# Attention and spectral mix on Trainium2: two batches of a head pair as one double unit

## The chip, the core and the metric

The kernel runs on one core of one Trainium2 chip. Its engines work side by side: PE (TensorE) multiplies and transposes, ACT (ScalarE) computes exponentials and copies out of PSUM, DVE (VectorE) multiplies and adds, POOL (GpSimd) casts, and SP (SyncE) issues the DMA transfers. The metric is the device time of one execution in microseconds (us). The median of the runs counts.

## What is computed

Windowed attention with a distance bias, then a mix in the frequency domain, then a residual with a matrix product. Eight batches, eight heads, 576 positions, head size 64, so the model width is 512.

```python
scores = scale * np.matmul(q, k.transpose(0, 1, 3, 2))
mask = (rel >= 0) & (rel < window)            # window = 128
scores = np.where(mask, scores + bias[None], -1000000000.0)
...
attn = attn / (np.sum(attn, axis=-1, keepdims=True) + 1e-09)
attn_out = np.matmul(attn, v)                 # becomes x: batch, position, 512
X = np.fft.rfft(x, axis=1)                    # the first 64 modes are used
Yr = np.einsum('bmd,mde->bme', Xr, w_r) - np.einsum('bmd,mde->bme', Xi, w_i)
Yi = np.einsum('bmd,mde->bme', Xr, w_i) + np.einsum('bmd,mde->bme', Xi, w_r)
y = np.fft.irfft(Y, n=S, axis=1)
u = x + y
out = u + np.maximum(u @ w_ch, 0.0)
```

Each of the 64 modes has its own 512 by 512 matrices w_r and w_i: 134 MB of weights against 28 MB of q, k and v.

## The kernel before

A **unit** is one pair of heads (index s, 0 to 3) of one batch b; there are 32. They go in two groups (GROUPS, line 19): the eight units of pair 0 first, then the 24 of pairs 1 to 3. The weights are split in the same way, by the rows that belong to a group's heads. Group 0's part (22 **weight tiles** of three modes, 768 KB of wr and as much of wi) is multiplied while the second group's attention is still running. The rest is streamed after the attention (lines 177 to 201), and the finish (`_finish`) transforms back and writes the result.

The order of the work on each engine is written by hand: instructions run on every engine in program order. The attention advances by **slots**, calls of `_slot` (lines 534 to 566), numbered n from 0. Slot n does, in this order: the first half of unit n's scores (`_score`, j = 0), the transposes of q and k of unit n+1 (`_tr`) and their copies out of PSUM on ACT (`_evac`), half of the slot's weight tiles (`_modes`), the transposes of unit n-1's v back to rows (`_vnat`, taken by DVE in `_vtake`), the second half of unit n's scores, the transposes of its v, casts to bf16 on POOL for the units to come (`_cast`, `_cast1`), one spectrum step (`_spectrum1`), the product of the weights of unit n-1 with v (`_av`), and the rest of the weight tiles. One score buffer, `sc`, serves both halves, so the second half waits until ACT has taken the exponential of the first. `_keep` (line 416) is a matmul that only keeps PE at work; it opens each unit's scores.

A transpose of q, k or v works on 64 by 64 blocks, one per head, at two positions of the array that can run side by side:

```python
for r in range(g.R):                          # 9
    for hh in range(2):
        hs = slice(64 * hh, 64 * hh + 64)
        g.nc.tensor.transpose(
            tp[hs, r, :], u.b[w][hs, r], g.ident_b[hs, hs], tile_position=(64 * hh, 64 * hh))
```

So a unit has 54 of them, and ten more in `_vnat`. The scores too run in two row halves of the array, one per head (lines 433 to 441).

All loads are issued by SP, in program order; an issue whose buffer is still in use holds up those behind it. q and k have QK = 9 buffers each, v has VB = 6, the weights a ring of RING = 3 tiles. 16 units are asked for ahead of slot 0 (n0, line 113), with the first three weight tiles between them. From slot 8 on, each slot asks for one unit more, then for one weight tile for each that it will use, three ahead (lines 154 to 163). Lines 144 to 153 spread the weight tiles of group 0 over slots 10 to 35: SHARE (4) is a slot's weight up to slot 23, SHARE_END (7) after it. w_ch comes in two loads of 0.5 MB into a buffer of its own (`wcp`, `_load_wch`).

Of the kernel before, what the change touches and what calls it, by code (L numbers as in the profile page):

```python
# [19 lines left out]
LA = 8  # L20
RING = 3
ROWS = 3
VB = 6
VN = 2
QK = 9
# [10 lines left out]
def kernel(  # L36
# [23 lines left out]
    g.units = units = [(j, s, b) for j, grp in enumerate(GROUPS) for b in range(B) for s in grp]  # L60
# [18 lines left out]
    g.W, g.unit, g.acc = {}, {}, {}  # L79
# [11 lines left out]
    with tc.manual_schedule(engines={ET.SP, ET.PE, ET.Activation, ET.DVE, ET.Pool}):  # L91
        with ExitStack() as wctx:
# [4 lines left out]
            with ExitStack() as actx:  # L97
# [4 lines left out]
                g.vns = [cp.tile([P, ST, 2, 72], BF16, name=f"vn{i}") for i in range(VN)]  # L102
                g.qpool = actx.enter_context(tc.tile_pool(name="qk", bufs=QK))
                g.vpool = actx.enter_context(tc.tile_pool(name="v", bufs=VB))
                g.wcp = actx.enter_context(tc.tile_pool(name="wcp", bufs=1))
# [7 lines left out]
                n0 = g.first[1] + LA  # L113
                for n in range(n0):
                    _load_unit(g, n)
                    if n < VB - 1:
                        _load_v(g, n)
                    elif n >= VB + 2:
                        _load_v(g, n - 3)
                    if g.first[1] - 1 <= n < g.first[1] - 1 + RING:  # L120
                        _load_w(g, 0, *todo.pop(0))
                with tc.tile_pool(name="tmpc", bufs=1, side="right") as tp:
                    _consts(g, tp)
                    _cast(g, 0)
                    _cast1(g, 0, 2)
                    _cast(g, 1)
                    for w in range(2):
                        _tr(g, 0, w)
                        _evac(g, 0, w)
                    first = list(dict.fromkeys(u[1] for u in units[:2]))  # L130
                    rest = [s for s in range(NP) if s not in first]
                    for s in first:
                        _mask(g, s)
                    for n in range(3):
                        _slot(g, n, [], [])
                    for s in rest:
                        _mask(g, s)
                zx = ctx.enter_context(tc.tile_pool(name="zx", bufs=1, side="right"))
                g.ZTa = zx.tile([P, 4, 2, NM, 8], FP32)
                loaded = n0  # L140

                line = [(j, *t) for j in range(len(GROUPS)) for t in tiles[j]]
                ahead = RING
                work = {n: [] for n in range(N + 2 + TAIL)}
                for j in range(len(GROUPS) - 1):
                    steps = []
                    for n in range(g.first[j + 1] + 2, g.first[j + 2] + 2):
                        steps += [n] * (SHARE if n < N - LA else SHARE_END)
                    if j + 2 == len(GROUPS):
                        steps += [n for n in range(N + 2, N + 2 + TAIL)] * SHARE_END  # L150
                    steps.sort()
                    for i, t in enumerate(tiles[j]):
                        work[steps[i * len(steps) // len(tiles[j])]].append((j, *t))
                for n in range(3, N + 2 + TAIL):
                    if g.first[1] <= n and loaded < N + 3:
                        if loaded < N:
                            _load_unit(g, loaded)
                        _load_v(g, loaded - 3)
                        loaded += 1
                    w = work[n]  # L160
                    for _ in w:
                        _load_w(g, *line[ahead])
                        ahead += 1
                    h = (len(w) + 1) // 2
                    _slot(g, n, w[:h], w[h:])
                    for i in range(2):
                        if n == g.first[1] + 4 + 8 * i:
                            _load_wch(g, i)
                        if n == g.first[1] + 10 + 8 * i:
                            _cast_wch(g, i)  # L170
# [105 lines left out]
def _mask(g, s):  # L276

    for h in (2 * s, 2 * s + 1):
        g.nc.scalar.activation(g.mask[:, h], g.rel, AF.Exp, scale=-(2.0 ** (-8.0 * (h + 1) / g.H)))
# [47 lines left out]
def _load_unit(g, n):  # L327
    nc = g.nc
    _, s, b = g.units[n]
    u = g.unit.setdefault(n, Ctx())  # L330
    u.q = g.qpool.tile([P, g.R, g.D], FP32, tag="q", name=f"q{n}")
    u.k = g.qpool.tile([P, g.R, g.D], FP32, tag="k", name=f"k{n}")
    for t, src in ((u.q, g.q), (u.k, g.k)):
        nc.sync.dma_start(
            out=t.rearrange("p r d -> p (r d)"),
            in_=src[b, 2 * s : 2 * s + 2].rearrange("h (p r) d -> (h p) (r d)", r=g.R))


def _load_v(g, n):

    _, s, b = g.units[n]
    u = g.unit.setdefault(n, Ctx())
    u.v = g.vpool.tile([P, g.R, g.D], FP32, tag="v", name=f"v{n}")
    g.nc.sync.dma_start(
        out=u.v.rearrange("p r d -> p (r d)"),
        in_=g.v[b, 2 * s : 2 * s + 2].rearrange("h (p r) d -> (h p) (r d)", r=g.R))


def _cast(g, n):
    u = g.unit[n]  # L350
    u.b, u.tp, u.T = [], [], []
    for w in range(2):
        _cast1(g, n, w)


def _cast1(g, n, w):
    u = g.unit[n]
    tb = g.work.tile([P, g.R, g.D], BF16, tag=f"b{w}", name=f"b{w}")
    g.nc.gpsimd.tensor_copy(tb, (u.q, u.k, u.v)[w])  # L359
    u.b.append(tb)  # L360
# [466 lines left out]
```

## Time and profile before

| what | time |
|---|---|
| median of 3 runs | 465.02 us (461.57 to 465.75) |
| the profiled execution | 463.15 us |
| its span, first to last instruction | 461.4 us |
| busy PE / PEld / DVE / ACT / POOL | 344.5 / 232.1 / 223.0 / 201.9 / 104.3 us |
| mean granted clock of PE | 0.748 of full speed |
| read from HBM, written | 163.58 MB, 9.44 MB |

The profile is of one execution. PEld is the loading of a matmul's stationary operand, which overlaps with PE. Busy shares are means over stages with different limits, so the stages have to be read apart. In lists of waits each row is: who waited, for whom, us in total, times, the longest. In the order of time a row is: start, duration, engine, line, operation, result and operands, shape, count, and in brackets how long the engine had been idle and what ended it; "issue" is a wait for nothing that the profile shows. Matmuls overlap one another, so a row of several is shorter than their durations added up.

### The profile page before, as it was taken

The page shows a single profiled execution, that of the slowest core. Times are in us where ns is not written, and L with a number is a line of the kernel's source. Part 1 is how long each engine was busy: PE and PEld are TensorE (multiplying, and loading weights), DVE is VectorE, ACT ScalarE, POOL GpSimd, SP SyncE. Part 2 cuts the span into 40 slices and gives each one's busy share as a digit, 9 for nine tenths or more (in the row PEclk, how much of TensorE's full clock was granted, in tenths as well). Part 3 has the DMA queues.
Part 4 walks back from the last instruction along what each step waited for, and adds up shares of the span by engine and source line. Part 5 has one row for each costly group of instructions (what it writes and reads, how often), then busy time and mean ns, then how long its engine had stood idle before and what let it go on. Part 6 is the DMA issues. An engine that isn't in the chain of part 4 may idle for free.

```text
span 461.4 us, 14063 instructions
## 1 busy us (share of the span) xinstructions
PE 344.5 (75%) x6082; PEld 232.1 (50%) x6110; DVE 223.0 (48%) x444; ACT 201.9 (44%) x316; POOL 104.3 (23%) x144
## 2 busy tenths in 40 slices
PE   3878989989889997656656655566565568879995
PEld 2556667767667765334434333334333345535553
DVE  7548765666666565324323133132232334511885
ACT  4988885767865571212232122122121223310884
POOL 6635453454544301000000000000000000000783
PEclk9989995787975597566585566565655759969999
DMA  8999889999998989999999999999999999994687
GB/s 299 396 405 394 308 307 402 381 400 341 361 350 310 358 289 329 413 425 423 423 422 425 421 424 423 424 423 422 426 423 424 425 423 393 422 423 198 226 311 285
DMA packets 55197, 173.92 MB, mean 377 GB/s; under 512 B 4960, under 2 KB 4960, under 8 KB 55136
## 3 DMA queue, kind: packets, MB, share of 16 engines
q1 hardware_dynamic: 55136, 173.03, 95.2%
q8 instruction: 47, 0.77, 0.6%
q14 instruction: 14, 0.11, 0.1%
HBM read 163.58 MB, written 9.44 MB: 375 GB/s over the span
## 4 chain that ended last, share of the span: by engine, by line
DMA 42%; PE 36%; ACT 8%; DVE 8%; issue 3%; SPq 1%; POOL 0%; ACTq 0%; POOLq 0%
DMA wi<-in_moe_w_i_dram 42%; PE acc L621 7%; PE tqk L370 6%; PE av L473 5%; PE sc L437 3%; ACT att L443 3%; PE xt L518 2%; PE mm L654 2%; DVE att L449 2%; ACT T L378 2%; PE sc L418 2%; PE y L654 2%; DVE x_sb L482 2%; PE av L402 2%; PE xw L667 1%
## 5 line engine op out<-in xcount | busy, mean ns | idle before, releaser
L671 ACT CAST hl<-xw 64x512 bf16<-64x512 f32 x72 | 41.8, 580 | 166.5 <-PE xw L667 122.7
L621 PEld LDWEIGHTS <-wi 128*128 128x128 bf16 x1024 | 65.4, 105 | 70.4 <-DMA wi<-in_moe_w_i_dram 68.9
L621 PE MATMUL acc<-Xlast,wi 128*128 128x16 bf16 x768 | 55.6, 193 | 52.0 <-DMA wi<-in_moe_w_i_dram 51.9
L672 DVE TENSOR_TENSOR hl<-xw,hl 64x512 bf16<-64x512 f32 x72 | 49.6, 689 | 82.6 <-ACT hl L671 82.5
L621 PEld LDWEIGHTS <-wr 128*128 128x128 bf16 x1024 | 69.4, 106 | 37.5 <-DMA wr<-in_moe_w_r_dram 26.5
L443 ACT ACTIVATE att<-sc 128x1024 bf16<-128x1024 f32 x64 | 66.2, 1034 | 41.0 <-PE sc L437 40.6
L793 POOL TENSOR_TENSOR o<-r,ys 128x512 f32<-128x512 f32 x18 | 22.5, 1277 | 246.5 <-DVE r L785 245.1
L621 PE MATMUL acc<-Xlast,wr 128*128 128x16 bf16 x768 | 62.8, 194 | 20.7 <-DMA wr<-in_moe_w_r_dram 14.8
L449 DVE TENSOR_TENSOR att<-att,mask 128x1024 bf16<-128x1024 bf16 x64 | 49.2, 769 | 45.7 <-ACT att L443 45.4
L378 ACT COPY T<-tqk 128x576 bf16<-128x576 bf16 x96 | 58.8, 649 | 1.0 <-PE tqk L370 1.0
L667 PE MATMUL xw<-wch,xT 128*128 128x512 bf16 x122 | 53.3, 564 | 4.9 <-issue 3.1
L370 PE MATMUL tqk<-ident_b,b 64*64 64x64 bf16 x1728 | 46.9, 209 | 7.7 <-POOL b L359 4.7
L370 PEld LDWEIGHTS <-b 64*64 64x64 bf16 x1728 | 39.5, 123 | 21.3 <-issue 11.7
L647 DVE COPY xT<-tp 128x512 bf16<-128x512 bf16 x36 | 15.2, 423 | 57.3 <-PE tp L645 57.0
L359 POOL CAST b<-q 128x576 bf16<-128x576 f32 x32 | 21.9, 685 | 59.2 <-PE tqk L370 40.1
L473 PE MATMUL av<-vn,att 128*128 128x65 bf16 (+1 forms) x576 | 31.8, 210 | 3.2 <-issue 2.5
L437 PE MATMUL sc<-T,T 64*128 64x256 bf16 (+2 forms) x320 | 30.1, 291 | 4.9 <-ACT att L443 4.4
L359 POOL CAST b<-k 128x576 bf16<-128x576 f32 x32 | 33.2, 1037 | 1.8 <-PE tqk L370 1.4
L667 PEld LDWEIGHTS <-xT 128*128 128x128 bf16 x144 | 19.0, 137 | 22.9 <-issue 20.6
L473 PEld LDWEIGHTS <-att 128*128 128x128 bf16 (+1 forms) x576 | 26.1, 110 | 8.0 <-issue 3.3
L359 POOL CAST b<-v 128x576 bf16<-128x576 f32 x32 | 21.6, 676 | 23.2 <-PE tqk L370 9.1
L482 DVE TENSOR_TENSOR x_sb<-av,rec 128x512 bf16<-128x512 f32 x32 | 22.1, 691 | 0.6
(98 smaller groups left out, 443.6 us busy)
## 6 DMA issues: line engine op xcount, KB each, us to landing
wr<-in_moe_w_r_dram SPq DMA_DIRECT2D x85, 768.0 KB, 8.3
wi<-in_moe_w_i_dram SPq DMA_DIRECT2D x85, 768.0 KB, 9.7
q<-in_q_dram SPq DMA_DIRECT2D x32, 288.0 KB, 7.0
k<-in_k_dram SPq DMA_DIRECT2D x32, 288.0 KB, 7.0
v<-in_v_dram SPq DMA_DIRECT2D x32, 288.0 KB, 7.4
out_dram<-o SPq DMA_DIRECT2D x32, 256.0 KB, 2.6
wchf<-in_moe_w_ch_dram SPq DMA_DIRECT2D x2, 512.0 KB, 8.8
out_dram<-o SPq DMA_DIRECT2D x8, 128.0 KB, 2.5
```

Of the source, the lines that this page charges most:

```text
L359: g.nc.gpsimd.tensor_copy(tb, (u.q, u.k, u.v)[w])
L370: g.nc.tensor.transpose(tp[hs, r, :], u.b[w][hs, r], g.ident_b[hs, hs], tile_position=(64 * hh, 64 * hh))
L378: g.nc.scalar.copy(dst.rearrange("c (p r) -> c p r", r=g.R), u.tp[w][:, 0 : g.R].rearrange("c r p -> c p r"))
L437: nc.tensor.matmul(sc[:, hh, c0 : c0 + nq], lhsT=kT[hs, _start(kt) : _start(kt) + P], rhs=qT[hs, kt * P : kt * P + nq], start=True, stop=T ...
L443: nc.scalar.activation(a, sc, AF.Exp, scale=1.0 / math.sqrt(g.D))
L449: nc.vector.tensor_tensor(out=a, in0=a, in1=m, op=ALU.mult)
L473: nc.tensor.matmul(av[o, hh, col(t)], lhsT=u.att[min(kt // 2, 1)][:, hh, c0 : c0 + m], rhs=u.vn[:, kt, hh, 0 : D + 1], start=(i == 0), sto ...
L482: nc.vector.tensor_tensor(out=xo, in0=avv[:, :, 0:4, 0:D], in1=rec[:, :, 0:4].unsqueeze(-1).broadcast_to([P, 2, 4, D]), op=ALU.mult)
L621: nc.tensor.matmul(acc[:, et, :, m - c0, :], lhsT=(wr, wi)[k][:, a].bitcast(BF16)[:, 1::2][:, et * P : (et + 1) * P], rhs=X[:, a, 1 - k : ...
L667: nc.tensor.matmul(xw, lhsT=xT[:, dt], rhs=g.wch[:, dt], start=(dt == 0 and g.way[n] != "q"), stop=(dt == 3))
L671: nc.scalar.copy(g.hl[hi, n, h], xw[hi])
L672: nc.vector.tensor_tensor(out=g.hl[lo, n, h], in0=xw[hi], in1=g.hl[hi, n, h], op=ALU.subtract)
```

## The change

Two units, the batches b and b+1 of the same pair of heads, become one **double** (index d, 0 to 15), and the list of units is ordered so that they are neighbours. A double takes two slots, n = 2d + e: slot e works on head e of the pair for both batches.

- q, k and v of the two batches are cast into one tile, side by side. Each transpose is then 128 by 128: both heads in the rows, both batches in the columns. A double has 27 instead of 108, in two parts per operand (5 and 4 of the 9), and ten instead of twenty in `_vnat`. The copies on ACT take 640 or 512 elements instead of 576.
- In the scores the two row halves of the array hold the two batches. `_keep` stands ahead of both halves in the even slot, and not in the odd one.
- `_av` works on the double before, two slots later than its scores instead of one. `_vnat` now comes after the second scores. The cast tiles have one buffer instead of two.
- Slot 2d casts q of double d+2, slot 2d+1 its k and v.
- Buffers: QK 7 (was 9), VB 5 (was 6). Nine doubles are asked for ahead of slot 0, a weight tile after each of the last three of them. From slot 8 on, each even slot asks for one double.
- The weight tiles of group 0 are spread over slots 11 to 35, with the larger share from slot 22; numbered from 0, tiles 0 to 10 are used in slots 11, 12, 14, 15, 17, 19, 20, 22, 23, 24, 24, then one in each slot, and none in slots 13, 16, 18 and 21. Tile i+3 is asked for in the slot that uses tile i.
- The masks of the eight heads, on ACT, come two ahead of slot 0 and then one after each slot. Double 0 is transposed whole before slot 0.
- w_ch comes in four loads of 256 KB into buffers of q and k that are no longer needed, in slots 24 to 30, cast four slots later. The buffer `wcp` goes.

```diff
-LA = 8
+LA = 10
 RING = 3
 ROWS = 3
-VB = 6
-VN = 2
-QK = 9
+VB = 5
+QK = 7
...
-    g.units = units = [(j, s, b) for j, grp in enumerate(GROUPS) for b in range(B) for s in grp]
+    g.units = units = [
+        (j, s, b) for j, grp in enumerate(GROUPS) for c in range(0, B, 2) for s in grp for b in (c, c + 1)]
...
-                n0 = g.first[1] + LA
-                for n in range(n0):
-                    _load_unit(g, n)
-                    if n < VB - 1:
-                        _load_v(g, n)
-                    elif n >= VB + 2:
-                        _load_v(g, n - 3)
-                    if g.first[1] - 1 <= n < g.first[1] - 1 + RING:
+                loaded = (g.first[1] + LA) // 2
+                for d in range(loaded):
+                    _load(g, d)
+                    if d >= loaded - RING:
                         _load_w(g, 0, *todo.pop(0))
...
-                    _cast(g, 0)
-                    _cast1(g, 0, 2)
-                    _cast(g, 1)
-                    for w in range(2):
-                        _tr(g, 0, w)
-                        _evac(g, 0, w)
-                    first = list(dict.fromkeys(u[1] for u in units[:2]))
-                    rest = [s for s in range(NP) if s not in first]
-                    for s in first:
-                        _mask(g, s)
-                    for n in range(3):
-                        _slot(g, n, [], [])
-                    for s in rest:
-                        _mask(g, s)
+                    for w in range(3):
+                        _cast(g, 0, w)
+                        for part in range(2):
+                            _tr(g, 0, w, part)
+                            _evac(g, 0, w, part)
+                    for w in range(3):
+                        _cast(g, 1, w)
+                    heads = list(range(H))
+                    for _ in range(2):
+                        _mask(g, heads.pop(0))
+                    n1 = 0
+                    while heads:
+                        _slot(g, n1, [], [])
+                        n1 += 1
+                        _mask(g, heads.pop(0))
...
+                start = g.first[1] + 3
+                steps = []
+                for n in range(start, N + 2 + TAIL):
+                    steps += [n] * (SHARE if n < N - LA else SHARE_END)
                 work = {n: [] for n in range(N + 2 + TAIL)}
-                for j in range(len(GROUPS) - 1):
-                    steps = []
-                    for n in range(g.first[j + 1] + 2, g.first[j + 2] + 2):
-                        steps += [n] * (SHARE if n < N - LA else SHARE_END)
-                    if j + 2 == len(GROUPS):
-                        steps += [n for n in range(N + 2, N + 2 + TAIL)] * SHARE_END
-                    steps.sort()
-                    for i, t in enumerate(tiles[j]):
-                        work[steps[i * len(steps) // len(tiles[j])]].append((j, *t))
-                for n in range(3, N + 2 + TAIL):
-                    if g.first[1] <= n and loaded < N + 3:
-                        if loaded < N:
-                            _load_unit(g, loaded)
-                        _load_v(g, loaded - 3)
+                for i, t in enumerate(tiles[0]):
+                    work[steps[i * len(steps) // len(tiles[0])]].append((0, *t))
+                for n in range(n1, N + 2 + TAIL):
+                    if g.first[1] <= n and n % 2 == 0 and 2 * loaded < N:
+                        _load(g, loaded)
                         loaded += 1
                     w = work[n]
                     for _ in w:
                         _load_w(g, *line[ahead])
                         ahead += 1
-                    h = (len(w) + 1) // 2
+                    h = (len(w) + 1) // 2 if n > start else 0
                     _slot(g, n, w[:h], w[h:])
-                    for i in range(2):
-                        if n == g.first[1] + 4 + 8 * i:
-                            _load_wch(g, i)
-                        if n == g.first[1] + 10 + 8 * i:
-                            _cast_wch(g, i)
+                    i, r = divmod(n - (N - LA + 2), 2)
+                    if 0 <= i < 4 and r == 0:
+                        _load_wch(g, i)
+                    if 2 <= i < 6 and r == 0:
+                        _cast_wch(g, i - 2)
...
+def _load(g, d):
+    _, s, b = g.units[2 * d]
+    u = g.two.setdefault(d, Ctx())
+    u.raw, u.b, u.T, u.att = [[], [], []], [None] * 3, [None] * 3, {}
+    for w, (pool, src) in enumerate(((g.qpool, g.q), (g.qpool, g.k), (g.vpool, g.v))):
+        for e in range(2):
+            t = pool.tile([P, g.R, g.D], FP32, tag="qkv"[w], name=f"{'qkv'[w]}{2 * d + e}")
+            g.nc.sync.dma_start(
+                out=t.rearrange("p r d -> p (r d)"),
+                in_=src[b + e, 2 * s : 2 * s + 2].rearrange("h (p r) d -> (h p) (r d)", r=g.R))
+            u.raw[w].append(t)
...
+def _cast(g, d, w):
+    u = g.two[d]
+    u.b[w] = g.work.tile([P, g.R, 2, g.D], BF16, tag=f"b{w}", name=f"b{w}", bufs=1)
+    for e in range(2):
+        g.nc.gpsimd.tensor_copy(u.b[w][:, :, e], u.raw[w][e])
+def _tr(g, d, w, part):
+    u = g.two[d]
+    r0, r1 = ((0, 5), (5, g.R))[part]
+    u.tp = g.ps1.tile([P, 5, P], BF16, tag="tqk", name=f"tqk{w}")
+    for r in range(r0, r1):
+        g.nc.tensor.transpose(
+            u.tp[:, r - r0], u.b[w][:, r].rearrange("p u d -> p (u d)"), g.ident_b)
+def _evac(g, d, w, part):
+    u = g.two[d]
+    r0, r1 = ((0, 5), (5, g.R))[part]
+    if part == 0:
+        u.T[w] = g.work.tile([P, 2, g.S], BF16, tag=f"T{w}", name=f"T{w}", bufs=1 if w == 2 else 2)
     g.nc.scalar.copy(
-        dst.rearrange("c (p r) -> c p r", r=g.R),
-        u.tp[w][:, 0 : g.R].rearrange("c r p -> c p r"))
-    u.T.append(dst)
+        u.T[w].rearrange("c h (p r) -> c (h p) r", r=g.R)[:, :, r0:r1],
+        u.tp[:, 0 : r1 - r0].rearrange("c r p -> c p r"))
...
+def _vnat(g, d, e, av):
+    u = g.two[d]
+    i0, n = ((0, 3), (6, 2))[e]
+    c0 = (4 + e) * (g.D + 1) + e
+    vt = av[:, :, c0 : c0 + n * g.D].bitcast(BF16)
+    for i in range(2 * n):
+        h, t = divmod(i0 + i, g.ST)
+        g.nc.tensor.transpose(
+            vt[:, i // n, (i % n) * P : (i % n) * P + P],
+            u.T[2][:, h, _start(t) : _start(t) + P], g.ident_b)
+    vn = g.vns[d % 2][:, i0 : i0 + 2 * n, :, 0 : g.D]
     g.nc.vector.tensor_copy(
-        u.vn[:, :, :, 0 : g.D].rearrange("p t h d -> p h t d"),
-        u.vt.rearrange("p h (t d) -> p h t d", t=g.ST))
+        vn.rearrange("p (k i) u d -> p k (i u) d", k=2),
+        vt.rearrange("p k (i d) -> p k i d", d=g.D))
...
+def _score(g, d, j, h):
+    nc = g.nc
+    u = g.two[d]
+    hd = 2 * g.units[2 * d][1] + h
+    qT, kT = u.T[0], u.T[1]
     sc = g.ps2.tile([P, 2, 512], FP32, tag="sc", name="sc")
+    if h == 0:
+        _keep(g, sc[:, 0])
+    parts = [(0, 0, 256), (1, 256, 256)] if j == 0 else [(2, 0, 256), (3, 256, 192), (4, 448, 64)]
+    for kt, c0, nq in parts:
+        for e in range(2):
+            es = slice(64 * e, 64 * e + 64)
+            nc.tensor.matmul(
+                sc[:, e, c0 : c0 + nq],
+                lhsT=kT[es, h, _start(kt) : _start(kt) + P],
+                rhs=qT[es, h, kt * P : kt * P + nq],
+                start=True, stop=True, tile_position=(64 * e, 0))
+    a = g.work.tile([P, 2, 512], BF16, tag=f"att{j}{h}", name=f"att{j}{h}")
+    nc.scalar.activation(a, sc, AF.Exp, scale=1.0 / math.sqrt(g.D))
+    u.att[j, h] = a
...
+def _av(g, d, e, av):
...
+    for h in range(2):
+        for t in range(4):
+            part(t, e, h, slice(0, P))
+    n = 4 + e
+    if e:
+        for h in range(2):
+            for f in range(2):
+                part(4, f, h, slice(64 * f, 64 * f + 64), tile_position=(0, 64 * f))
...
+    N = len(g.units) // 2
+    d, e = divmod(n, 2)
+    here, nxt, old = d < N, d + 1 < N, 0 <= d - 1 < N
+    if here:
+        _score(g, d, e, 0)
+    if nxt:
+        _tr(g, d + 1, e, e)
+        _evac(g, d + 1, e, e)
     for w in w0:
         _modes(g, *w)
-    if 0 <= n - 1 < N:
-        av = _av_tile(g)
-        _vnat(g, n - 1, av)
-        _vtake(g, n - 1)
-    if n < N:
-        _score(g, n, 1)
-        _tr(g, n, 2)
-        _evac(g, n, 2)
-    if n + 2 < N:
-        _cast(g, n + 2)
-    if n + 1 < N:
-        _cast1(g, n + 1, 2)
-    if 0 <= n - 2 < N:
-        _spectrum(g, n - 2)
-    for t in range(1 if n <= N else len(g.spectra)):
+    if here:
+        _score(g, d, e, 1)
+    if e == 0 and nxt:
+        for w, part in ((0, 1), (1, 0)):
+            _tr(g, d + 1, w, part)
+            _evac(g, d + 1, w, part)
+    av = g.ps2.tile([P, 2, 512], FP32, tag="av", name="av") if here or old else None
+    if here:
+        _vnat(g, d, e, av)
+    if e == 1 and nxt:
+        for part in range(2):
+            _tr(g, d + 1, 2, part)
+            _evac(g, d + 1, 2, part)
+    if d + 2 < N:
+        for w in ((0,), (1, 2))[e]:
+            _cast(g, d + 2, w)
+    if e == 0 and 0 <= d - 2 < N:
+        _spectrum(g, d - 2)
+    for t in range(len(g.spectra) if d > N else 1):
         if g.spectra:
             _spectrum1(g, *g.spectra.pop(0))
-    if 0 <= n - 1 < N:
-        _av(g, n - 1, av)
+    if old:
+        _av(g, d - 1, e, av)
...
+    t = g.qpool.tile([P, g.R, g.D], FP32, tag="qk"[i % 2], name=f"wchf{i}")
+    g.wchf = getattr(g, "wchf", []) + [t.rearrange("p r d -> p (r d)")[:, 0 : g.DM]]
+    g.nc.sync.dma_start(out=g.wchf[i], in_=g.w_ch[P * i : P * i + P])
 def _cast_wch(g, i):
-    g.nc.gpsimd.tensor_copy(g.wch[:, 2 * i : 2 * i + 2], g.wchf)
+    g.nc.gpsimd.tensor_copy(g.wch[:, i], g.wchf[i])
...
```

## The prediction

> **What bounds the kernel now.** I read the 40 slices first, then busy time by stage, then what PE waited for, then the order of single instructions. A slot is one call of `_slot`; I time slots by the one keep-warm matmul (L418) that opens each.
>
> ```profile
> PE   3878989989889997656656655566565568879995
> PEclk9989995787975597566585566565655759969999
> DMA  8999889999998989999999999999999999994687
> GB/s 299 396 405 394 308 307 402 381 400 341 361 350 310 358 289 329 413 425 423 423 422 425 421 424 423 424 423 422 426 423 424 425 423 393 422 423 198 226 311 285
> ```
>
> ```profile
> 30.20:63.98 33.78, 30.11 (x825) 22.39 (x823) 25.78 (x60) 28.45 (x41) 18.67 (x24) 0.98 0.91 338
> 63.98:127.75 63.77, 58.46 (x1344) 43.15 (x1343) 41.38 (x91) 44.87 (x64) 29.27 (x37) 0.79 1.00 378
> 127.75:182.00 54.25, 50.47 (x1088) 37.71 (x1086) 32.91 (x76) 30.32 (x44) 14.10 (x17) 0.71 0.92 329
> 182.00:424.00 242.00, 157.41 (x2138) 98.34 (x2163) 76.64 (x134) 50.03 (x89) 2.47 (x16) 0.65 1.00 414
> 424.00:461.40 37.40, 30.34 (x312) 18.00 (x308) 27.55 (x43) 25.58 (x46) 22.54 (x18) 1.00 0.70 254
> ```
>
> The rows are slots 4 to 11, slots 12 to 23, slots 24 to the last weights of group 0, the streamed weights, and the finish; columns: window, length, busy PE, PEld, DVE, ACT, POOL, granted clock, DMA share, GB/s. From 182 to 424 us the DMA runs at its ceiling, so the end moves one for one with the moment the last group-0 weights are used (182.0). Before that PE is the bound: 93% busy, and nearly without data waits:
>
> ```profile
> PE av L473 <- issue: 2.5, 3, 1.3
> PE tqk L370 <- issue: 2.0, 2, 1.6
> PE xt L518 <- issue: 1.3, 1, 1.3
> PE av L402 <- DVE x L485: 1.2, 3, 0.8
> PE acc L621 <- issue: 0.7, 1, 0.7
> ```
>
> These are all PE waits above 0.3 us from 55 to 178 us (total, times, longest). None is for weights. "Issue" adds to 6.5 us, and cutting windows at the stalls tells what it is:
>
> ```profile
> 66.88:97.58 30.70, 28.80 (x640) 0.72 1.03 394
> 97.58:116.34 18.76, 17.65 (x384) 0.73 0.96 364
> 126.27:132.19 5.92, 4.59 (x128) 1.00 1.04 393
> 132.19:169.61 37.42, 36.44 (x769) 0.64 0.90 316
> ```
>
> The stalls lie 640, 384, 128 and 769 matmuls apart, multiples of 128 but for one record: 128 matmuls with their loads are 256 instructions, so PE waits for code. The clock follows: after stalls of 1.61, 1.26 and 1.33 us it fell to 0.5 (at 69, 99, 133 us), after 0.72 and 0.81 us it stayed. It was 0.5 for 15.6, 10.6 and 27.8 us. A slot with one weight tile takes 4.31 us at full clock (118.85 to 123.16) and 6.47 at half (76.23 to 82.70).
>
> **The change, part by part.**
>
> *Transposes.* Durations of a run of them:
>
> ```profile
> 52.00 0.75 PE L370 MATMUL tqk<-ident_b,b 64*64 64x64 bf16 x36
> 83.78 1.17 PE L370 MATMUL tqk<-ident_b,b 64*64 64x64 bf16 x36
> 190.57 0.59 PE L645 MATMUL tp<-ident_b,x_sb 128*128 128x128 bf16 x4
> 380.26 0.38 PE L645 MATMUL tp<-ident_b,x_sb 128*128 128x128 bf16 x4
> ```
>
> One takes 217 ns alone at full clock, 311 at half, so each further one adds (0.75-0.217)/35 = 15 ns (64x64, full), 25 ns (half), and for 128x128 (0.38-0.217)/3 = 55 ns (full), 93 ns (half). A double had 108 small ones plus 20 for v (13 and 21 ns); it gets 27 plus 10 large ones. Net of tile switches that is 1.9 before, 2.0 us after at full clock; 3.1 and 3.4 at half. A quarter of the instructions, no less time. What goes is the pause where a 64x64 run meets another tile shape: 36 of them start 0.68 us ahead of the weights (0.56 net), 1.10 at half (0.89 net).
>
> PE by start-to-start times, two slots with one weight tile each (full / half): keep 0.64/1.08, first scores 0.64/1.08, q/k/v transposes 2.14/3.44, weights 1.68/1.72, v back 0.30/0.52, second scores 0.66/1.10, spectrum 1.00/1.52, A times V 1.54/2.48: 8.60/12.94, which are the measured slots. After: transposes 27 x 0.055 = 1.49 (2.51), v back 0.55 (0.93), the rest the same in number: 8.20/12.42.
>
> *A wait in the slot.* From the first scores to the second is 1.51 us through ACT's exp (L437 at 123.48, exp at 123.92, L437 at 124.99). Before, 36 transposes and v back filled it; now 4 or 5 transposes (0.25) do. With a weight tile (0.84) the hole is 0.1 us a slot, without one about 0.9. A full-clock slot becomes 4.2 us with or without weights (before 4.31, and 4.0 to 4.4 without). At half clock: 6.2 for 6.47 with, 6.1 for 5.5 (6.47 less its weights) without. Over slots 12 to 31, in the mix before (8 weight slots at full, 8 at half, 4 without): -1.0, -2.1, +0.5 = **-2.6 us**.
>
> *ACT, DVE, POOL.* Evacuations move the same elements in as many instructions (640 or 512 for 576, 0.59 us apart); rec and x4 lose one each per double. ACT's slot stays 2 x 0.94 + 3 x 0.59 = 3.65, under 4.2: hidden. If the five-element runs cost as much as an exp (0.94), ACT needs 4.7 and a slot grows 0.5; I take the copy's own row. Casts become strided: six at 0.67 to 1.18 are 4 to 7 us of 8.4, one slot ahead: hidden either way.
>
> *Code.* A double issues 91 matmuls and 91 loads fewer. Slots 12 to 31 fall from some 18 blocks of 128 to 11, the 6.5 us of stalls by 38%: **-2.5 us**. The Trainium skill, "Runtime: NRT & Kernel Launch", Instruction fetch mechanics, gives the same 256-instruction block and calls its cost mostly hidden; by it this term would be 0 and the sum 2.5 us higher. The trace differs: 6.5 us.
>
> *Loads on SP.* SP issues in program order. With VB 5 for 6, v of unit u waits for the cast of unit u-5, and that cast now comes at the end of an odd slot: double D's second v goes out late in slot 2D-7. Weight tiles queue behind it. D=15, the last, sits in the program at slot 20, but its v waits for the cast late in slot 23; tile 9 behind it is used in slot 24. wr and wi go out 0.5 us apart after the v; v plus tile are 1.87 MB, 4.4 us at 424 GB/s, and with some 2.5 us to start (wr's quickest landing is 4.4 us for 0.79 MB) wi lands 5.4 us after PE wants it. Tile 10 then meets its use, tile 11 is 0.7 (half clock) to 2.3 us late: 6.1 to 8.0, taken **+7 us**. Tiles 3, 4, 5 and 8 (used in slots 15, 17, 19, 23; released two slots earlier) are 1.1 us late at full clock, on time at half: 0 to 4.4, taken **+2 us**. Behind a stalled weight matmul PE's second scores, v and A times V stand, and ACT and DVE with them.
>
> *Start and tail.* Six casts and six evacuations before slot 0 (from 7.01, 0.6 each), the table load 1.28 and two masks 1.15 put the first exp at 13.1 instead of 11.39; in return the six masks in one piece, behind which PE waited 2.1 us at 27, are spread. At 4.3 a slot the exp of slot 12 is due at 64.7 (before 64.72): **0**, within 2 either way. Six spectra now come in slot 34, three in slot 33 before: **+1**. w_ch is the same 1 MB in four issues and four casts, on queues idle by then: 0, and if late 1 us.
>
> *Clock.* Share at 0.5 left as it is: **0**.
>
> Sum: -2.6 - 2.5 + 7 + 2 + 0 + 1 = +4.9. The profiled execution took 463.15 (span 461.4), 1.9 below the median 465.02, so 468 against it and 470 against the median. 1% is about what a measurement here can tell.
>
> **The rivals.**
>
> *The clock stays up (faster).* Fewer code blocks, fewer drops. If slots 12 to 23 keep full clock, 26.2 us at half become 17.5: -8.7, 461. If it also recovers at once after slot 24, DMA sets the rest: thirteen tiles, 20.4 MB, 48 us plus the start instead of 59: 453. It decides in the slots before 24, where the new holes are 1.1 us: above 0.81 (kept) and below 1.26 (dropped). I take 457. In its favour: 38% fewer blocks; against: the tail's tiles are as dense as those that held 0.5 for 27.8 us. The Trainium skill, "TensorE: Matmul & The Clock Gate", Why this matters for your kernels, lets only gaps over some 3 us drop the clock, and by that the first half stays up. The trace had drops after 1.3.
>
> *The clock stays down (slower still).* Both keep-warm matmuls now lie in even slots. All of slots 12 to 23 at half: 12 x 6.2 = 74 against some 64: 480.
>
> *The weights are not held up.* If v casts free buffers a slot earlier, or tiles land within 4 us, +9 falls to about 2: 463. For it: no weight wait now; against: the program order.
>
> **How the numbers follow.** Forecast, 470, own range 465 to 475: 0.48. Clock up, 457: 0.26. Clock down, 480: 0.14. No hold-up, 463: 0.12. Faster by over 1% (below 460.4): most of the second, 0.23. Within 1% (to 469.7): the last, the upper rest of the second, and about a third of the forecast: 0.32. Slower: 0.45. Leaving out the outer tenths: 455 to 481.
>
> **What would show it.** PE waits for wi of 5 us near slot 24, SP held by POOL's b; long "issue" waits at fewer places; 128x128 transposes 55 ns apart; slots of 4.2 us without weights; DMA lulls ahead of slots 13, 15, 17. The forecast is wrong if PE never waits for weights in the attention, if the clock's share there leaves 0.7 to 0.8, or if ACT's copies take longer than 0.7 us.

## The result and the profile after

The changed kernel takes 492.40 us (median of 4 runs, 491.98 to 493.12), the kernel before on the same chip 465.38: a ratio of 1.060 (95% interval 1.053 to 1.066), 27 us slower. The forecast was 470 with a range of 455 to 481: right in sign, wrong in size and, as the runs below show, wrong in the main cause.

The slices of the changed kernel (span 490.7 us, mean clock 0.715), to be held against those of before:

```profile
PEclk9957676577778777557756656666555668978998
GB/s 311 395 204 187 254 306 249 168 320 283 362 338 311 407 405 340 308 344 423 424 425 423 423 423 424 424 422 422 423 425 423 423 425 413 423 421 288 150 314 309
```

The clock falls at 27 us and stays at half until 40; before, it dipped only from 28 to 31. From 25 to 123 us the DMA moves 168 to 320 GB/s, where before it moved 307 to 405. By stage (slots 4 to 11, slots 12 to 23, slots 24 to the last weights of group 0, streamed weights; the columns are those of the prediction):

```profile
34.27:82.40 48.13, 38.75 (x448) 28.23 (x445) 27.67 (x50) 32.34 (x42) 18.59 (x24) 0.69 0.71 249
82.40:152.52 70.12, 56.63 (x806) 42.94 (x803) 38.33 (x69) 47.95 (x64) 27.75 (x36) 0.76 0.80 287
152.52:216.52 64.00, 52.34 (x769) 39.98 (x765) 31.11 (x63) 29.91 (x40) 11.41 (x16) 0.66 0.99 367
216.52:453.00 236.48, 155.72 (x2123) 97.50 (x2148) 77.37 (x135) 50.03 (x89) 2.47 (x16) 0.66 1.00 416
```

Measured from one opening keep-warm matmul to another, the time moved as follows. The last column shares out the terms of the forecast by stage; the prediction itself gives only their sum.

| stage | before | after | difference | forecast |
|---|---|---|---|---|
| start to slot 4 | 30.2 | 34.3 | +4.1 | 0 |
| slots 4 to 11 | 33.8 | 48.1 | +14.3 | 0 |
| slots 12 to 23 | 63.8 | 70.1 | +6.3 | about -1 |
| slot 24 to the last group-0 weights | 54.5 | 64.0 | +9.5 | about +6 |
| streamed weights and finish | 279.2 | 274.2 | -5.0 | 0 |

Half of the loss lies in slots 4 to 11, where the prediction expected none: seven of the eight have no weight tile at all. What PE waited for from 30 to 217 us (total, times, longest):

```profile
PE av L434 <- DVE vn L377: 20.0, 17, 1.8
PE sc L403 <- ACT att L409: 8.8, 15, 0.8
PE acc L596 <- DMA wi<-in_moe_w_i_dram: 3.0, 2, 1.7
PE acc L596 <- DMA wr<-in_moe_w_r_dram: 2.1, 1, 2.1
```

The first row is all but new (0.6 us in two waits before): A times V (`_av`) waits for DVE's copy of v's transposes (in `_vnat`). The second is the wait for exp that the prediction costed. DVE's own order in slot 5, one row an instruction, tells why the first is so long, and the PE row shows its end:

```profile
42.17 1.18 DVE L417 TENSOR_TENSOR att<-att,mask 128x1024 bf16<-128x1024 bf16 x1 [0.77 <-ACT att L409]
43.69 1.07 DVE L417 TENSOR_TENSOR att<-att,mask 128x1024 bf16<-128x1024 bf16 x1 [0.34 <-ACT att L409]
44.68 0.41 DVE L377 COPY vn<-av 128x512 bf16<-128x512 bf16 x1
46.02 0.22 DVE L450 RECIPROCAL rec<-av 128x10 f32<-128x10 f32 x1 [0.93 <-PE av L434]
```

```profile
45.14 0.83 PE L434 MATMUL av<-vn,att 128*128 128x65 bf16 x22 [1.34 <-DVE vn L377]
45.91 0.39 PE L384 MATMUL sc<-F,ident_b 128*32 128x512 bf16 x1
```

In the kernel before, the copy stood between the two mask products, here in its slot 5:

```profile
36.54 1.18 DVE L449 TENSOR_TENSOR att<-att,mask 128x1024 bf16<-128x1024 bf16 x1
37.75 0.49 DVE L411 COPY vn<-av 128x640 bf16<-128x640 bf16 x1
38.47 0.69 DVE L449 TENSOR_TENSOR att<-att,mask 128x1024 bf16<-128x1024 bf16 x1 [0.23 <-ACT att L443]
```

In the changed kernel PE had v's transposes ready by 42.9. But the copy was written behind `_score(g, d, e, 1)`, so in DVE's queue it stands behind the second mask product, which waits for the second exp (42.63 to 43.66). The slot has become one chain: scores, exp, mask product, copy of v, A times V, then the next slot's scores. ACT's first exp of slot 5 starts at 41.12 and that of slot 6 at 46.66: 5.54 us for a slot without weights at full clock, against 4.0 to 4.4 before.

The A times V that waits uses v of the double *before*; what it shares with the copy is only the PSUM tile `av`, in other columns. The Trainium skill, "PSUM — Partial Sum Buffer", PSUM bank collisions raise a hardware error, calls two engines at once in one bank and quadrant an error even at different columns; no run here shows that. That the shared tile makes the wait is read from the kernel; no run gave the copy a tile of its own.

### The profile page after: what moved, and what is told of

It is laid out like the page before. It is cut to its first block, busy times and chain, and to the rows that moved or that the text cites. A ratio compares the mean times of both kernels' runs of the same rounds, so it can differ in the third digit from the quotient of the medians.

```text
span 490.7 us, 10976 instructions
## 1 busy us (share of the span) xinstructions
PE 354.6 (72%) x4626; PEld 240.8 (49%) x4654; DVE 220.8 (45%) x396; ACT 211.9 (43%) x316; POOL 103.9 (21%) x146
## 4 chain that ended last, share of the span: by engine, by line
DMA 36%; PE 36%; ACT 15%; DVE 8%; issue 3%; SPq 1%; POOL 0%; ACTq 0%; POOLq 0%
DMA wi<-in_moe_w_i_dram 36%; ACT att L409 9%; PE acc L596 6%; PE av L434 6%; PE sc L403 5%; DVE att L417 4%; ACT T L354 3%; PE tqk L345 3%; PE sc L384 2%; PE xt L488 2%; PE mm L629 2%; PE idle L574 2%; PE xw L642 2%; DVE vn L377 2%; PE y L629 2%
## 5 line engine op out<-in xcount | busy, mean ns | idle before, releaser
L596 PEld LDWEIGHTS <-wi 128*128 128x128 bf16 x1024 | 65.4, 105 | 68.4 <-DMA wi<-in_moe_w_i_dram 67.2
L596 PEld LDWEIGHTS <-wr 128*128 128x128 bf16 x1024 | 69.9, 106 | 38.3 <-DMA wr<-in_moe_w_r_dram 26.8
L417 DVE TENSOR_TENSOR att<-att,mask 128x1024 bf16<-128x1024 bf16 x64 | 53.2, 831 | 66.4 <-ACT att L409 66.4
L354 ACT COPY T<-tqk 128x640 bf16<-128x640 bf16 x96 | 67.2, 751 | 0.9 <-PE tqk L345 0.3
L345 PE MATMUL tqk<-ident_b,b 128*128 128x128 bf16 x432 | 48.8, 272 | 6.9 <-POOL b L335 5.7
L345 PEld LDWEIGHTS <-b 128*128 128x128 bf16 x432 | 35.7, 123 | 19.7 <-issue 10.7
L403 PE MATMUL sc<-T,T 64*128 64x256 bf16 (+2 forms) x320 | 32.5, 309 | 13.1 <-ACT att L409 12.8
L434 PEld LDWEIGHTS <-att 128*128 128x128 bf16 (+1 forms) x576 | 28.0, 121 | 26.3 <-issue 22.3
L335 POOL CAST b<-q 128x576 bf16<-128x576 f32 x32 | 25.9, 836 | 54.9 <-issue 51.8
L335 POOL CAST b<-k 128x576 bf16<-128x576 f32 x32 | 24.2, 785 | 34.6 <-issue 34.4
L403 PEld LDWEIGHTS <-T 64*128 64x128 bf16 x320 | 14.4, 103 | 27.1 <-issue 24.7
L335 POOL CAST b<-v 128x576 bf16<-128x576 f32 x32 | 23.9, 773 | 14.9 <-POOL b L335 8.2
```

Source lines behind the costliest of these rows:

```text
L335: g.nc.gpsimd.tensor_copy(u.b[w][:, :, e], u.raw[w][e])
L345: g.nc.tensor.transpose(u.tp[:, r - r0], u.b[w][:, r].rearrange("p u d -> p (u d)"), g.ident_b)
L354: g.nc.scalar.copy(u.T[w].rearrange("c h (p r) -> c (h p) r", r=g.R)[:, :, r0:r1], u.tp[:, 0 : r1 - r0].rearrange("c r p -> c p r"))
L403: nc.tensor.matmul(sc[:, e, c0 : c0 + nq], lhsT=kT[es, h, _start(kt) : _start(kt) + P], rhs=qT[es, h, kt * P : kt * P + nq], start=True, s ...
L417: nc.vector.tensor_tensor(out=a, in0=a, in1=m, op=ALU.mult)
L434: nc.tensor.matmul(av[o, h, t * (D + 1) : (t + 1) * (D + 1)], lhsT=u.att[min(kt // 2, 1), h][:, f, c0 : c0 + m], rhs=vn[:, g.ST * h + kt, ...
```

## The experiments

Theory A: the place of v's copy in the order makes the chain, and the chain makes most of the loss. Theory B: the loads behind v on SP, as forecast, starve the slots. Theory C: the two-batch form itself, with ACT's shorter write runs, is the slower one. All ratios are against runs of the kernel before on the same chip.

**vn_first.** v's transposes and their copy go back ahead of the second scores.

```diff
+    av = g.ps2.tile([P, 2, 512], FP32, tag="av", name="av") if here or old else None
+    if here:
+        _vnat(g, d, e, av)
     if here:
         _score(g, d, e, 1)
...
-    av = g.ps2.tile([P, 2, 512], FP32, tag="av", name="av") if here or old else None
-    if here:
-        _vnat(g, d, e, av)
```

> The changed kernel, with v's transposes back to rows and DVE's copy of them put ahead of the second scores, as the kernel before had them; nothing else differs. Theory (the slot has become one serial chain: exp, the mask product, then DVE's copy of v behind it in DVE's queue, then A times V, which waits for that copy): A times V no longer waits for the copy, 20 slots lose about 1.2 us each, and with the 1.3 us holes gone the clock drops less: 464 to 472 us, slots without weights 4.2 to 4.5 us at full clock. Rival (the longer ACT copies of five-element runs set the slot): at most 5 us faster, 487 or more. Rival (loads held up on SP): the wait is elsewhere, 489 to 493.

Measured: 466.63 us, ratio 1.004 (1.0005 to 1.008): 25.8 us of the 27 are gone with one block moved up. DVE in slot 5 now, from its timeline:

```profile
37.10 0.71 DVE L417 TENSOR_TENSOR att<-att,mask 128x1024 bf16<-128x1024 bf16 x1 [0.70 <-ACT att L409]
37.73 0.41 DVE L377 COPY vn<-av 128x512 bf16<-128x512 bf16 x1
38.61 0.85 DVE L417 TENSOR_TENSOR att<-att,mask 128x1024 bf16<-128x1024 bf16 x1 [0.46 <-ACT att L409]
```

The copy stands between the two mask products; A times V starts at 38.44 with no wait, and slots 4 to 7, which have no weights, take 4.0 to 4.4 us, as before. In exchange v's transposes now wait for DVE's x of the slot before, which reads the same tile `av`: 5.3 us in slots 4 to 11. Theory A holds. Slots 12 to 23 take 63.4 us, and slot 24 to the last weights 59.3, 4.9 more than before. The hold-up on SP is still there: from 30 to 190 us PE waits 18.2 us for weights, where the changed kernel had 5.1. Slots 4 to 11 show in what coin the chain was paid:

```profile
30.54:66.32 35.78, 28.96 (x449) 20.36 (x444) 29.05 (x52) 32.87 (x45) 18.21 (x25) 1.00 0.91 328
```

Against the changed kernel's 48.13 they are 12.4 us shorter. PE's idle time is only 2.6 of that (6.8 for 9.4); the other 9.8 is the same 450 matmuls busy for 29.0 us instead of 38.75, at a clock of 1.00 instead of 0.69. The holes cost little themselves; what the lower clock adds is nearly four times as much.

**v_late.** Only that: v is asked for two doubles after q and k, much as the kernel before asked for it three units later.

```diff
+                    if d < 2:
+                        _load_v(g, d)
+                    elif d >= 4:
+                        _load_v(g, d - 2)
...
-                    if g.first[1] <= n and n % 2 == 0 and 2 * loaded < N:
-                        _load(g, loaded)
+                    if g.first[1] <= n and n % 2 == 0 and 2 * loaded < N + 4:
+                        if 2 * loaded < N:
+                            _load(g, loaded)
+                        _load_v(g, loaded - 2)
                         loaded += 1
```

> The changed kernel, with only the loads of v moved: each double's v is asked for two doubles later on SP, when its buffers are free, so that nothing queues behind it. Theory of the serial slot: the stall of 4 us at slot 24 and that of 1 us at slot 25 go and the slots stay as long as they are, so 485 to 489 us. Rival (the hold-up on SP starves the attention all along): 470 or less, and the early slots get shorter too.

Measured: 485.77 us, ratio 1.043 (1.037 to 1.049), 6.6 us under the changed kernel, as expected. The hold-up is real. In the changed kernel it is one row of SP's waits and two rows of its timeline, that of SP and that of PE:

```profile
SPq L324 <- POOL b L335: 81.1, 14, 9.0
```

```profile
150.86 0.33 SPq L324 DMA_DIRECT2D v<-in_v_dram  x1
```

```profile
157.65 0.20 PE L596 MATMUL acc<-X,wi 128*128 128x16 bf16 x1 [1.73 <-DMA wi<-in_moe_w_i_dram]
```

SP stands 81 us in all for POOL's casts, and its timeline has gaps of 5 to 9 us between the two v's of a double. That total is not the price: in v_late SP still waits 69 us for casts, now with q and k. What changes is the weights behind them: PE's waits for weights from 30 to 217 us fall from 5.1 us to 0.5. In the changed kernel the last v goes out at 150.86, 1.7 us ahead of slot 24, with wr and wi of tile 9 behind it; slot 24 then lasts 10.4 us and slot 25 7.1. But the loss in slots 4 to 11 is as it was (46.8 us), so theory B explains the smaller part alone.

**both.** The two edits together; `both` is the name of this kernel below.

```diff
+    if here:
+        _vnat(g, d, e, av)
     if here:
         _score(g, d, e, 1)
...
+                        _load_v(g, loaded - 2)
                         loaded += 1
```

> The changed kernel with both mends: v's transposes back and their copy ahead of the second scores, and v's loads two doubles later on SP. If the serial slot and the hold-up on SP are two separate losses, the second is worth at least its 6.6 us again, and more, because with shorter slots the weights came late by 19.6 us in all in the first mend alone: 448 to 456 us, faster than the kernel before, with waits of PE for weights under 6 us before 190 us. Rival (the DMA ceiling sets the rest, so that the weights are late whatever stands ahead of them): 460 to 466, with the waits for weights kept.

Measured: 452.11 us, ratio 0.9735 (0.969 to 0.978): faster than before by 13 us. Its slices and stages (slots 12 to 23; slot 24 to the last weights):

```profile
PEclk9999899999869955666856666565565669969999
```

```profile
67.11:116.09 48.98, 45.04 (x805) 33.45 (x802) 37.86 (x68) 46.88 (x64) 23.64 (x34) 1.00 1.02 386
116.09:175.56 59.47, 47.22 (x771) 34.95 (x765) 30.80 (x64) 30.41 (x42) 12.75 (x18) 0.77 1.04 404
```

Slots 12 to 23 run at full clock throughout: 4.08 us each, 49.0 in all against 63.8 before. So the doubled form is not slower in itself, and theory C falls as the cause of the loss. The effects do not add: v_late is worth 6.6 us while the chain is there and 14.5 (466.63 to 452.11) without it. The waits for weights fit a reason: 5.1 us in the changed kernel and 18.2 in vn_first, so a chain that holds PE also gives late weights time to arrive. The expectation of under 6 us of such waits failed: 10.6 us are left in `both` up to 176 us, all of them from slot 24 on.

**dve_order.** Is it the place on DVE or on PE? Here PE's order is the changed kernel's; only the second mask product goes behind the copy in DVE's queue.

```diff
     u.att[j, h] = a
-    m = g.mask[:, hd]
+    if h == 0:
+        _mult(g, d, j, h)
+def _mult(g, d, j, h):
+    nc = g.nc
+    a = g.two[d].att[j, h]
+    m = g.mask[:, 2 * g.units[2 * d][1] + h]
...
     if here:
         _vnat(g, d, e, av)
+        _mult(g, d, e, 1)
```

> The changed kernel with one thing moved: in DVE's queue the copy of v stands ahead of the second mask product of its slot, in place of behind it. PE's order is the changed kernel's: v's transposes stay behind the second scores. If the wait of A times V behind exp and the mask product is the loss, this gives about what the first mend gave: 462 to 470 us. If it was PE's order (v's transposes no longer fill the wait for exp), most of the loss stays: 482 or more.

Measured: 471.27 us, ratio 1.011 (0.999 to 1.022). 21 of the 26 us are DVE's order alone. The wait for the copy shrinks to this (30 to 200 us):

```profile
PE av L440 <- DVE vn L377: 3.9, 12, 0.7
```

**order_late.** dve_order with v_late's loads.

```diff
+        _mult(g, d, e, 1)
...
+                        _load_v(g, loaded - 2)
                         loaded += 1
```

> The same with v's loads two doubles later on SP as well. By the theory of two separate losses it lands with the kernel with both mends, 448 to 456 us; as v's transposes need not wait here for DVE to empty the last slot's product (9.4 us of waits in the kernel with both mends), it may be up to 4 us below it. If PE's order matters it stays above 460.

Measured: 459.11 us, ratio 0.985 (0.976 to 0.995), between the two expectations, and 12.2 us under dve_order: with DVE's queue in order, the late v is again worth twice the 6.6 us. The 7 us that remain to `both` are what PE's own order is worth. Of these 4.3 come ahead of slot 4, which opens at 34.2 for 29.9. From slot 4 to slot 23 PE waits 8.9 us for exp and 3.7 for the copy; in `both` it waits 0.9 for exp, and 8.2 for DVE's x with v's transposes. So v's transposes in part fill the wait for the first exp.

**old_vn_last.** The converse, in the kernel before: the second scores go ahead of v's transposes.

```diff
     for w in w0:
         _modes(g, *w)
+    if n < N:
+        _score(g, n, 1)
     if 0 <= n - 1 < N:
         av = _av_tile(g)
         _vnat(g, n - 1, av)
         _vtake(g, n - 1)
     if n < N:
-        _score(g, n, 1)
         _tr(g, n, 2)
```

> The kernel before, with only v's transposes back and DVE's copy of them moved behind the second scores, as in the changed kernel. Theory of the serial slot: its slots without weights grow from 4.0 to about 5.4 us, and the whole takes 482 to 495 us, so this order alone accounts for most of the loss. Rival (128x128 transposes or the copies make it): 463 to 469.

Measured: 520.69 us, ratio 1.117 (1.110 to 1.124). The same move makes the same chain in the single-unit kernel, at a higher price than expected. From its waits (30 to 200 us) and DVE's timeline:

```profile
PE av L473 <- DVE vn L411: 30.6, 24, 1.8
```

```profile
59.25 0.85 DVE L449 TENSOR_TENSOR att<-att,mask 128x1024 bf16<-128x1024 bf16 x1 [1.14 <-ACT att L443]
60.13 0.49 DVE L411 COPY vn<-av 128x640 bf16<-128x640 bf16 x1
```

What was mis-sized in the expectation is the clock: most of these slots run at half clock (mean of the run 0.653), so even a slot without weights takes 6.8 us (slots 4 to 11, clock 0.50).

**evac_runs.** ACT's copies out of PSUM, with the order of the elements changed: PSUM is read in unbroken runs, and SBUF is written in single elements nine apart, where the changed kernel writes runs of five or four.

```diff
-        u.T[w].rearrange("c h (p r) -> c (h p) r", r=g.R)[:, :, r0:r1],
-        u.tp[:, 0 : r1 - r0].rearrange("c r p -> c p r"))
+        u.T[w].rearrange("c h (p r) -> c r (h p)", r=g.R)[:, r0:r1],
+        u.tp[:, 0 : r1 - r0])
```

> The changed kernel, with ACT's copies out of PSUM walking the same elements in the other order: PSUM read in runs of 128, SBUF written with a step of nine. If the five-element runs are what made a copy 750 ns, one of 640 elements falls to about 0.70 us and one of 512 to 0.60, 32 slots win 0.2 to 0.3 us each where ACT lies on the chain: 484 to 488 us. If the written step costs the same, no change, 490 to 494. By the theory of the serial slot no more than 8 us are in it either way.

Measured: 612.22 us, ratio 1.315 (1.308 to 1.322), far outside the expectation: the written step costs much more. The groups of ACT's copies (total us, mean ns), first of the changed kernel, then of evac_runs:

```profile
L354 ACT COPY T<-tqk 128x640 bf16<-128x640 bf16 x48 | 36.7, 765 | 0.9 <-PE tqk L345 0.3
L354 ACT COPY T<-tqk 128x512 bf16<-128x512 bf16 x48 | 35.3, 736 | 0.0
```

```profile
L354 ACT COPY T<-tqk 128x640 bf16<-128x640 bf16 x48 | 162.6, 3387 | 0.0
L354 ACT COPY T<-tqk 128x512 bf16<-128x512 bf16 x48 | 135.5, 2824 | 0.0
```

3387/640 = 5.3 ns for a single element written apart. Runs of five cost 765/128 = 6.0 ns a run and runs of four 736/128 = 5.8: a run costs nearly what one lone element costs, so the 512-element copy is hardly shorter than the 640. That fits what the change cost here: a pair of copies has 1152 elements as before, but takes 765 + 736 = 1501 ns, where two copies with unbroken writes took 2 x 649 = 1298.

**both_dve.** Does ACT bound the repaired kernel? One copy in six goes to DVE.

```diff
-    g.nc.scalar.copy(
+    (g.nc.vector.tensor_copy if (w, part) == (2, 1) else g.nc.scalar.copy)(
```

> As the kernel with both mends, and one of the six copies of a double out of PSUM (the second part of v, 512 elements) on DVE in place of ACT. If ACT is now the bound of slots without weights (two exps at 0.93 and three copies at 0.68 are 3.9 us, the slot measured in the first mend), those slots fall to 3.6 to 3.8 us and the whole by up to 5 us. If DVE, whose queue then has this copy between its products, holds up PE instead, the slots grow and it is slower by 2 us or more.

Measured: 453.55 us, ratio 0.977 (0.971 to 0.982), no gain over `both` (452.11). PE's largest wait becomes that of the tile `av` for DVE's x (9.2 us in all, 4.3 in `both`). The test is one-sided: it loads DVE with what it takes off ACT, so it doesn't show that ACT is free.

**both_keep.** A test of the keep-warm matmul, with an error in its expectation. The diff reads as if `_keep` stood before both halves of the even slot and none of the odd one. But the last argument of `_score` is the head: slot e works on half e of the scores, for both heads in turn, not on head e, and `if h == 0` puts one keep-warm matmul at the head of *each* slot (40.36 and 45.91 us open slots 5 and 6). The description of the change, the rival "the clock stays down" and this expectation have it wrong. The edit in truth bunches what was spread, two in the even slot and none in the odd:

```diff
-    if h == 0:
+    if j == 0:
         _keep(g, sc[:, 0])
```

> As the kernel with both mends, and the keep-warm matmul once in each slot, ahead of the first scores, in place of twice in the even slot and never in the odd one; their number is the same. If the bunched matmuls let the clock fall, the granted clock before 190 us rises by 0.05 or more and the time falls by 3 us or more. If holes of over a microsecond alone make it fall, the clock stays within 0.03 and the time within 2 us of the kernel with both mends, less about 0.3 us in each even slot at most, where the second of the two stood right after the wait for exp.

Measured: 454.18 us, ratio 0.979 (0.974 to 0.984): 2.1 us more than `both`, within what the intervals leave open. The clock from 60 to 120 us is 1.00 in both kernels. So in a slot without holes it hardly matters where this matmul stands.

**both_share.** A larger weight share up to slot 21, to have fewer tiles left at the end.

```diff
-SHARE, SHARE_END = 4, 7
+SHARE, SHARE_END = 6, 7
```

> The kernel with both mends and the weight tiles of group 0 spread more evenly over its slots (share 6 in place of 4 up to slot 21). The transfers fall to 278 GB/s from 55 to 75 us because the three tiles of the ring are waiting to be used, and are at their ceiling after that. If the ceiling after 75 us is what ends the attention, using the first tiles earlier frees the ring in that lull: 1 to 4 us faster. If not, the same within 1.5 us.

Measured: 450.06 us, ratio 0.970 (0.962 to 0.979). It is the fastest of all that ran, but the 2 us to `both` are inside the intervals.

## Why the prediction was wrong, point by point

**"A wait in the slot" (-2.6): this step failed.** It followed the second scores to ACT's exp and stopped. That wait is there in the size given (0.79 us each, 8.8 in all, against 0.9). What the step left out is what else stands behind the second scores once v's transposes are moved past them: DVE's copy, queued behind the second mask product, and A times V, which waits for the copy. By dve_order this is worth 21 us, by vn_first 26. The prediction said that v and A times V stand behind a stalled weight matmul, so the order was seen, but it never asked what A times V waits for.

**"ACT, DVE, POOL: hidden" failed with it.** The busy time was right: DVE has 38.3 of 70.1 us in slots 12 to 23. Being little busy says nothing about the place in a queue. ACT's copies were to take no longer than before (0.65 us each, 0.59 apart); they took 0.74 and 0.77, and past 0.7 the forecast had called itself wrong. ACT is busy with them 67.2 us for 58.8. Slots 4 to 11 take 37.2 us in `both` for 33.8 before, and the 3.4 come from two slots. In slot 8 (6.3 for 4.0) PE waits 1.5 us for DVE's x, behind a spectrum step in DVE's queue, and some 3 us at half clock follow. In slot 11 (6.1 for 4.2) the first weight tile comes last and waits 0.8 us for DVE.

**"Loads on SP" (+9): right.** The place (slots 24 and 25), the cause (POOL's casts) and the DMA lulls came as said; PE's waits there are 2.1, 1.7 and 1.3 us. v_late gives 6.6 us, within what the chain hides; without the chain it is 12 to 15, so the term was sound to small.

**"Code" (-2.5): too small.** No "issue" wait above 0.3 us is left in the attention of the changed kernel or of `both`: all 6.5 us are gone, not 38% of them, though `both` moves 386 GB/s in slots 12 to 23, for 378 before. By the Trainium skill, "Runtime: NRT & Kernel Launch", Instruction fetch mechanics, such cost is mostly hidden; that fits the kernels after and not the one before. What decides it was not tried.

**"Transposes": right.** Nine of 128x128 take 0.67 us, (0.67 - 0.217)/8 = 57 ns each for 55. With the chain gone, slots 12 to 23 of `both` take 4.08 us on the mean, with a weight tile or without, for 4.2. (PE's share before 182 us is 89, 92 and 93% by the stage rows, not 93% throughout; nothing hangs on it.)

**"Start and tail".** The first exp came at 13.75 for 13.1. The +4.1 up to slot 4 comes with the new place of v's transposes: in vn_first and `both` slot 4 opens at 30.5 and 29.9, for 30.2 before, so the 0 was right without it. DVE's order is not enough there, as slot 4 opens at 32.5 in dve_order and at 34.2 in order_late. That the streamed part would follow one for one was 5 us off: from the last group-0 product to the first with a streamed wi it is 4.0 us before and 1.2 after, and the stream itself takes 237.8 and 235.6. Nine of the doubled kernels show 273.6 to 275.4 us for this part, both_share 277.6; why was not tried.

**"Clock" (0) and the rivals.** The term of 0 fell with the wait: the clock went from 0.98 to 0.69 in slots 4 to 11, and that is most of the price there. The prediction had the rule of size for it (holes of 1.26 us drop the clock, those of 0.81 do not) and counted only the exp's holes. Nor does the rule hold: a hole of 1.39 us ahead of 62.73 in the changed kernel and one of 1.54 ahead of 50.01 in vn_first left the clock at 1.00, while one of 1.34 ahead of 68.03 and, in `both`, one of 1.52 ahead of 49.40 were followed by half clock. What decides between them is open. "The clock stays up" (457) is what comes true once the holes are gone: 1.00 in slots 12 to 23 of `both`, and 452. "The clock stays down" (480) is nearest in time, but for the wrong reason: the place of the keep-warm matmuls was misread, and it put the loss in slots 12 to 23. "The weights are not held up" is refuted by v_late. No rival had the chain.

## What to carry to other kernels

When a step is moved in a hand-written order, list for each engine what it is now queued behind, and follow the first instruction that needs its result: a 0.4 us copy cost 21 us because it came after a product that waits for exp. Ask this first of engines with low busy shares, since their totals hide it. And before giving up a change that lost, undo its order alone: here the new form was good for 3% once two orders were put back.

## What was not expected of the hardware

ACT's writes: a bf16 element written 18 bytes from the last costs 5.3 to 5.5 ns (3387/640, 2824/512), a run of five 6.0 (765/128). The Trainium skill, "Advanced Engine Details and Errata", SBUF Cachelines, says full speed needs at least two hits in a line of 16 bytes. The runs agree in kind, and give the price.

The clock: its mean in slots 4 to 11 was 0.69, with PE busy 38.75 of 48.13 us. It was still at half from a hole of 1.77 us at 27; later it fell after holes of 1.34 ahead of 45.14 and 68.03, with others of 0.5 to 0.8 between them. The Trainium skill, "TensorE: Matmul & The Clock Gate", Why this matters for your kernels, puts the limit at gaps of some 3 us. In this case holes of about half that were enough, though not each time. With the chain gone it was 0.99 in dve_order, 1.00 in vn_first and 0.95 in `both` in the same slots.
